# Raw load buffers of a fused linear-attention and feed-forward kernel: rows of 512 bytes instead of 384, three buffers instead of four

## The chip, the cores and the metric

The kernel runs on one core of one Trainium2 chip. The metric is device time in microseconds (us) of one execution. The engines are named as in the profile: PE (TensorE matmul) and PEld (its weight load), DVE (VectorE), ACT (ScalarE), POOL (GpSimd), and SP (SyncE), which here only issues DMAs.

## The reference

The kernel computes a gated linear attention and then a feed-forward layer with a squared ReLU. q, k, v and alpha have shape (4 batches, 8 heads, 768 tokens, 48 channels) in float32; the output is (3072, 384) in float32.

```python
for t in range(S):
    state = alpha[:, :, t, :, None] * state + einsum('bhd,bhe->bhde', k[:, :, t], v[:, :, t])
    y[:, :, t] = einsum('bhd,bhde->bhe', q[:, :, t], state)
x = y.transpose(0, 2, 1, 3).reshape(B * S, H * D)
h = maximum(x @ w_in, 0.0)          # w_in 384 x 2048
out = (h * h) @ w_out               # w_out 2048 x 384
```

## The kernel before, in words

**Tiles.** The work is cut into 12 tiles, numbered g = 0 to 11, of 256 tokens of one batch each. Tiles 0 to 3 are the first parts of the four batches, 4 to 7 the second, 8 to 11 the third. Partition p of the 128 holds the token pair 2p and 2p+1.

**Loads.** For each tile, `load(g)` (L494 to L511) issues four DMAs of 384 KB, for alpha, k, q and v, into one of the raw buffers `RAW` (L378). Such a buffer has, for each partition, the four quantities, each with 8 heads, each with 2 tokens of 48 channels in float32, so that a head has a row of 2 x 48 x 4 = 384 bytes. In HBM the heads of one partition lie far apart, each as a run of 384 bytes. SP issues the loads of all tiles but tile 2, whose four come from POOL (`POOL_LOADS`, L365), as do the four weight loads (`win` and `wout`, L480). Tile g uses buffer g modulo `NRAW` (L367), which is 4.

**What a load waits for.** Three things gate a load: (1) `AFTER` (L1044 to L1046): an earlier transfer must have landed, from tile 4 on the previous tile's q; (2) from tile 5 on, `BEHIND` (L492): an instruction of the previous tile must be done, its Ln for alpha, its k product for k, its transpose for q and v; (3) the buffer must be free: the instructions that read the same part of it for the tile `NRAW` tiles earlier must be done.

**Front of a tile.** `front_by_heads` (tile 0) and `front` (the other tiles) read the raw buffer:
- alpha: Ln on ACT (L525, L587, `la` at L658), the pair product `prd` on DVE or POOL (L616, L618), further products (L645, L654). Cumulated decays come from a TensorE product and Exp on ACT.
- k and q: multiplied with the decays on DVE into `qks` (L561, L687, L692).
- v: cast to bfloat16 into `vbf`, by ACT (L683) or POOL (L554, L682). These two places hold the lines `vin, vout = ...` (L553, L681).

`qks` is then transposed, on TensorE for tiles 0 to 2 and by DMA (L703, issued by SP) from tile 3 on.

**The rest of a tile.** `scores` (L881, masked by DVE at L892), `state` (L752, with L847 to L858) and `output` (L773, L784, L813, L820) make the attention's result `xbf`, which is transposed to `xt` (L927 on TensorE, L933 by DMA). `moe` runs the feed-forward layer: the first product at L983, ReLU at L991 or L993, the square at L1001 or L1005, the second product at L1018, its copy out of PSUM at L1025 or L1027, and a store at L1034. The very last half tile is at L953 to L961. L1068 is filler: TensorE products of zeros in idle time at the start.

**The order of the work.** A list scheduler written in Python (`Program.schedule`) plays the operations through with assumed costs and due times, picks an engine where an operation has alternatives (`alts`), and so fixes the order of instructions on each engine while the kernel is built. `Program.place` turns the dependencies into semaphore waits and drops those that another wait already implies. On the chip each engine runs its list in order, each instruction after its waits.

Of the kernel before, what the change touches and what calls it, by code (L numbers as in the profile page):

```python
# [8 lines left out]
FP32 = mybir.dt.float32  # L9
# [24 lines left out]
class Program:  # L34
# [23 lines left out]
    def add(self, eng, fn, cost, prio, reads=(), writes=(), name="", dma=None, lag=0, after=(), mode=("F", "F"),  # L58
            alts=None):

        reads, writes = ([h for k in keys for h in ((k + (0,), k + (1,)) if len(k) == self.HALVED.get(k[0]) else (k,))]
                         for keys in (reads, writes))
        choices = {eng: (fn, cost)}
        if alts:
            choices.update(alts)
        op = Op(choices, prio, name)
        op.idx = len(self.ops)
        op.lag = lag
        op.mode = mode
        if dma is not None:  # L70
            if dma not in self.dma_sems:
                self.dma_sems[dma] = self.nc.alloc_semaphore("d_" + dma)
                self.dma_count[dma] = 0
            self.dma_count[dma] += 1
            op.sem = (dma, self.dma_count[dma])
        for o in after:
            op.deps[o] = True
        for k in reads:
            w = self.writer.get(k)
            if w is not None:  # L80
                op.deps[w] = True
            if k[0] == "ps":
                for r in self.readers.get(k, ()):
                    op.deps.setdefault(r, False)
        for k in writes:
            w = self.writer.get(k)
            if w is not None:
                op.deps[w] = True
            for r in self.readers.get(k, ()):
                if r is not op:  # L90
                    op.deps.setdefault(r, False)
        for k in reads:
            self.readers.setdefault(k, []).append(op)
        for k in writes:
            self.writer[k] = op
            self.readers[k] = []
        op.deps.pop(op, None)
        self.ops.append(op)
        return op
# [227 lines left out]
def act_ns(n):  # L327
    return 180 + n * 0.8333
# [10 lines left out]
def bass_gla_recurrent__then__act_relu_squared_kernel(  # L339
# [9 lines left out]
    B, H, S, D = q.shape  # L349
# [14 lines left out]
    DENSE = {0: 19172, 1: 35978, 2: 46351, 3: 61182, 11: 160500}  # L364
    POOL_LOADS = {2: "akqv"}  # L365
    RATIO = 4
    NRAW, NQKS, NKQT, NPM, NV, NXT, NGT, NRR, NOSB = 4, 3, 3, 2, 4, 4, 2, 4, 2  # L367
    WS = 2
    LATE_STATE = (1, 2)
    ROW_TILED = tuple(range(PE_TRANSPOSED, G))  # L370
# [4 lines left out]
    def sb(name, shape, dt, n):  # L375
        return [nc.alloc_sbuf_tensor(f"{name}{i}", shape, dt) for i in range(n)]

    RAW = sb("raw", [128, 4, H, 2, D], FP32, NRAW)  # L378
    PRD = sb("prd", [128, HD], FP32, 2)
    LA1 = sb("la1", [128, HD], FP32, 2)  # L380
    LAB = sb("lab", [128, H, 64], BF16, 2)
# [7 lines left out]
    VBF = sb("vbf", [128, H, 2, D], BF16, NV)  # L389
# [104 lines left out]
    def load(g):  # L494
# [7 lines left out]
        for j, t, nm in ((0, alpha, "a"), (1, k, "k"), (2, q, "q"), (3, v, "v")):  # L502
            src = t[b, :, t0:t0 + T, :].rearrange("h (p j) d -> p h (j d)", j=2)
            dst, key = RAW[r][:, j], ("raw", r, j)
            ring, cost, gate = "sp", 600, AFTER.get((g, nm), AFTER.get(g))
# [7 lines left out]
    def front_by_heads(g, p0):  # L513

        r, la, qs, kt, vb = (g % n for n in (NRAW, 2, NQKS, NKQT, NV))
        N = HD // 2

        def lanes(t, x):
            return t[la][:].rearrange("p j (x n) -> p j x n", x=2)[:, :, x]

        for x in range(2):
# [3 lines left out]
            add("act", lambda e, hs=hs: e.activation(LAF[la][:, :, hs, 0:D].rearrange("p j h d -> p h j d"),  # L525
                RAW[r][:, 0, hs], AF.Ln), act_ns(HD) + 30, px + 100, reads=[("raw", r, 0, x)], writes=[("laf", la, x)],
                name=f"ln{x}_{g}")
# [22 lines left out]
            add("act", lambda e, x=x, bank=bank: e.activation(ACM[la][:, 4 * x:4 * x + 4], bank[:, HD:HD + 4], AF.Exp),  # L550
                act_ns(4), p0 + 560 + x, reads=key, writes=[("acm", la, x)], name=f"ec{x}_{g}")

        vin, vout = RAW[r][:, 3].rearrange("p h j d -> p (h j d)"), VBF[vb][:].rearrange("p h j d -> p (h j d)")  # L553
        add("pool", lambda e: e.tensor_copy(vout, vin), 830, p0 + 900, reads=[("raw", r, 3)], writes=[("vbf", vb)],  # L554
            name=f"vc{g}", alts={"act": (lambda e: e.activation(vout, vin, AF.Copy), act_ns(2 * HD))})

        for x in range(2):
            hs = slice(4 * x, 4 * x + 4)
            px = p0 + 40 * x
            for a, E, nm in ((0, EK, "ek"), (1, EQ, "eq")):  # L560
                add("dve", lambda e, a=a, E=E, hs=hs, x=x: e.tensor_tensor(  # L561
                    QKS[qs][:, a, :, hs, 0:D], RAW[r][:, 1 + a, hs].rearrange("p h j d -> p j h d"),
                    lanes(E, x).rearrange("p j (h d) -> p j h d", h=4), ALU.mult), dve_ns(HD), px + 1500 + 10 * a,
# [20 lines left out]
    def decays_by_token(g, p0, r, la):  # L584

        bank, keys = (psX, [("ps", "X", 0), ("ps", "X", 1)]) if g == 0 else (psWH, [("ps", "W"), ("ps", "H", 0)])
        add("act", lambda e: e.activation(LAF[la][:, :, :, 0:D].rearrange("p j h d -> p h j d"), RAW[r][:, 0], AF.Ln),  # L587
            act_ns(2 * HD) + 30, p0 + 100, reads=[("raw", r, 0)], writes=[("laf", la)], name=f"ln{g}")
# [22 lines left out]
    def decays_by_pair(g, p0, r, la, last):  # L611

        def al(j):
            return RAW[r][:, 0, :, j, :]

# [49 lines left out]
    def front(g):  # L665
        b, i = units[g]
        t0 = i * T
        p0 = FRONT.get(g, (g - 1) * P)
        if g in BY_HEADS:
            front_by_heads(g, p0)  # L670
            return
        r, la, qs, kt, pm, vb, x2 = (g % n for n in (NRAW, 2, NQKS, NKQT, NPM, NV, 2))
        first, last = i == 0, i == NST - 1
        sr, sw = 2 * b + i % 2, 2 * b + (i + 1) % 2

        if g in BY_TOKEN:
            decays_by_token(g, p0, r, la)
        else:
            decays_by_pair(g, p0, r, la, last)

        vin, vout = RAW[r][:, 3].rearrange("p h j d -> p (h j d)"), VBF[vb][:].rearrange("p h j d -> p (h j d)")  # L681
        add("pool", lambda e: e.tensor_copy(vout, vin), 830, p0 + 900, reads=[("raw", r, 3)], writes=[("vbf", vb)],  # L682
            name=f"vc{g}", alts={"act": (lambda e: e.activation(vout, vin, AF.Copy), act_ns(2 * HD))})  # L683

        for j in range(2) if g in ROW_TILED else ():
            dst = QKS[qs][:, 1].rearrange("p j h d -> p (j h d)").rearrange("p (n j x d) -> p j n x d", n=NPR, j=2, x=2)[:, j, :, :, 0:D]
            add("dve", lambda e, j=j, dst=dst: e.tensor_tensor(  # L687
                dst, RAW[r][:, 2, :, j, :].rearrange("p (n x) d -> p n x d", x=2),
                EQ[la][:, j].rearrange("p (n x d) -> p n x d", n=NPR, x=2), ALU.mult),
                dve_ns(HD), p0 + 1600 + j, reads=[("raw", r, 2), ("eq", la, j)], writes=[("qks", qs, 1, j)], name=f"eqm{j}_{g}")  # L690
        for a, E, key in ((0, EK, "ek"), (1, EQ, "eq"))[:1 if g in ROW_TILED else 2]:
            add("dve", lambda e, a=a, E=E: e.tensor_tensor(  # L692
                QKS[qs][:, a, :, :, 0:D], RAW[r][:, 1 + a].rearrange("p h j d -> p j h d"),
                E[la][:].rearrange("p j (h d) -> p j h d", h=H), ALU.mult),
                dve_ns(2 * HD), p0 + 1500 + 100 * a, reads=[("raw", r, 1 + a), (key, la, 0), (key, la, 1)],
                writes=[("qks", qs, a)], name=f"{key}m{g}")

        if g in ROW_TILED:

            for c in range(2):  # L700
                src = QKS[qs][64 * c:64 * c + 64].rearrange("p a j h d -> p (a j h d)")
                dst = transposed(kt, c).rearrange("p (b s) -> p b s", s=64)
                add("sp", lambda e, dst=dst, src=src: e.dma_start_transpose(dst, src), 1300, p0 + 2500 + c,  # L703
                    reads=[("qks", qs, 0), ("qks", qs, 1)], writes=[("kqt", kt, 0, c), ("kqt", kt, 1, c)], name=f"tr{c}_{g}",
                    dma=f"t{c}_{kt}", lag=1700)
            return

        for a in range(2):
            src = QKS[qs][:, a].rearrange("p j h d -> p (j h d)")
            bank = psZ[:, a, :].bitcast(BF16)  # L710
            psk = [("ps", "Z", a)]

            def tr(pe, src=src, bank=bank):
                for o in range(2 * NPR):
                    ins = pe.matmul(bank[:, o * 128:(o + 1) * 128], src[:, o * 128:(o + 1) * 128], IDENT[:],
                                    is_transpose=True)
                return ins

            add("pe", tr, pe_ns(8, 128), p0 + 2500 + a, reads=[("qks", qs, a), ("ident",)], writes=psk,
                name=f"tr{a}_{g}")  # L720
            dst = KQT[kt][:, a].rearrange("p j n s -> p (j n s)")
            add("dve", lambda e, dst=dst, bank=bank: e.tensor_copy(dst, bank[:, 0:1024]), dve_ns(1024, 2),
                p0 + 3000 + a, reads=psk, writes=[("kqt", kt, a)], name=f"et{a}_{g}",
                alts={"act": (lambda e, dst=dst, bank=bank: e.activation(dst, bank[:, 0:1024], AF.Copy),
                              act_ns(1024))})
# [374 lines left out]
```

## Time and profile before

| | |
|---|---|
| Time, three runs | 176.28, 176.63, 177.08 us; median 176.63 |
| Profiled execution | span 174.5 us from the first to the last instruction, 5086 instructions; its time beyond the span is not recorded by itself |
| PE busy | 167.6 us (96%) |
| PEld busy | 129.9 us (74%) |
| DVE busy | 121.7 us (70%) |
| ACT busy | 118.9 us (68%) |
| POOL busy | 15.3 us (9%) |
| SP's DMA queue (q1) | 73,184 packets, 28.32 MB, 72.3% of the 16 DMA engines' span |
| POOL's DMA queue (q0) | 1,536 packets, 4.72 MB, 12.2% |
| Raw loads from SP | 44 of 384 KB; median time from issue to landing 3.6 us (alpha), 4.4 (k), 4.0 (q), 4.8 (v) |

How to read it: the profile comes from one execution, seen by the hardware profiler. A group of instructions is named by its line, its engine and "output <- inputs" by the program's tensors, without buffer numbers. "Idle before" is idle time of an engine ahead of these instructions, with what ended it. PE's busy time is modelled from pipelined matmuls, so a busy PE is not necessarily a PE at its peak. SPq is SP's list of DMA issues; an issue can last long when the DMA queues are full.

### The profile page before, as it was taken

The page shows a single profiled execution, that of the slowest core. Times are in us where ns is not written, and L with a number is a line of the kernel's source. Part 1 is how long each engine was busy: PE and PEld are TensorE (multiplying, and loading weights), DVE is VectorE, ACT ScalarE, POOL GpSimd, SP SyncE. Part 2 cuts the span into 40 slices and gives each one's busy share as a digit, 9 for nine tenths or more (in the row PEclk, how much of TensorE's full clock was granted, in tenths as well). Part 3 has the DMA queues.
Part 4 walks back from the last instruction along what each step waited for, and adds up shares of the span by engine and source line. Part 5 has one row for each costly group of instructions (what it writes and reads, how often), then busy time and mean ns, then how long its engine had stood idle before and what let it go on. Part 6 is the DMA issues. An engine that isn't in the chain of part 4 may idle for free.

```text
span 174.5 us, 5086 instructions
## 1 busy us (share of the span) xinstructions
PE 167.6 (96%) x2233; PEld 129.9 (74%) x2235; DVE 121.7 (70%) x201; ACT 118.9 (68%) x211; POOL 15.3 (9%) x24
## 2 busy tenths in 40 slices
PE   7998988999999989999999999999999999999994
PEld 2566887856787669778778878878788797688773
DVE  5597959596958599978869958958769726322230
ACT  3863689777769669578679759669578564566440
POOL 3160840020002002000200000000000000000000
PEclk9999999999999999999999999999999999999999
DMA  5999999989999899899999998899999690040022
GB/s 144 324 296 197 259 307 214 236 213 313 210 226 174 215 232 190 209 246 193 258 199 183 258 193 207 225 191 264 248 186 209 112 187 4 0 135 4 10 80 90
DMA packets 74742, 33.36 MB, mean 191 GB/s; under 512 B 71648, under 2 KB 71904, under 8 KB 74720
## 3 DMA queue, kind: packets, MB, share of 16 engines
q1 hardware_dynamic: 73184, 28.32, 72.3%
q0 software_dynamic: 1536, 4.72, 12.2%
q8 instruction: 17, 0.28, 0.7%
q14 instruction: 5, 0.04, 0.1%
HBM read 25.17 MB, written 4.72 MB: 171 GB/s over the span
## 4 chain that ended last, share of the span: by engine, by line
PE 62%; DMA 27%; SPq 4%; DVE 2%; ACT 2%; POOL 1%; issue 1%
PE psWH L983 27%; PE psO L1018 26%; DMA win<-in_moe_w_in_dram 7%; DMA raw<-in_q_dram 7%; DMA raw<-in_alpha_dram 5%; DMA wout<-in_moe_w_out_dram 4%; DMA raw<-in_v_dram 4%; SPq L509 3%; PE psX L784 2%; PE psX L773 2%; PE psX L953 2%; PE psX L881 1%; PE psZ L752 1%; DVE pm L892 1%; PE psZ L881 1%
## 5 line engine op out<-in xcount | busy, mean ns | idle before, releaser
L983 PE MATMUL psWH<-xt,win 128*128 128x256 bf16 x576 | 73.6, 274 | 1.5 <-DMA win<-in_moe_w_in_dram 1.0
L983 PEld LDWEIGHTS psWH<-xt,win 128*128 128x128 bf16 x576 | 65.2, 145 | 6.5 <-issue 0.8
L1018 PE MATMUL psO<-wout,gt 128*128 128x384 bf16 x368 | 69.4, 326 | 0.1
L991 ACT ACTIVATE rr<-psWH 128x512 bf16<-128x512 f32 x80 | 47.3, 595 | 23.0 <-PE psWH L983 21.4
L1018 PEld LDWEIGHTS psO<-wout,gt 128*128 128x128 bf16 x368 | 34.7, 98 | 18.2 <-ACT osb L1025 0.3
L1001 DVE TENSOR_TENSOR gt<-rr 128x1024 bf16<-128x1024 bf16 (+1 forms) x43 | 25.6, 597 | 24.7 <-ACT rr L991 24.4
L892 DVE TENSOR_TENSOR pm<-psX,caus 128x1024 bf16<-128x1024 f32 x12 | 14.6, 1218 | 0.9 <-PE psZ L881 0.9
L892 DVE TENSOR_TENSOR pm<-psZ,caus 128x1024 bf16<-128x1024 f32 x12 | 14.6, 1218 | 0.8 <-PE psZ L881 0.8
L1005 ACT ACTIVATE gt<-rr 128x512 bf16<-128x512 bf16 (+1 forms) x17 | 14.1, 828 | 0.5
L912 ACT ACTIVATE xbf<-psX 128x768 bf16<-128x768 f32 x12 | 9.7, 810 | 6.4 <-PE psX L773 5.4
L1025 ACT ACTIVATE osb<-psO 128x384 f32<-128x384 f32 x19 | 9.3, 492 | 5.7 <-PE psO L1018 5.1
L993 DVE TENSOR_SCALAR rr<-psWH 128x512 bf16<-128x512 f32 x16 | 11.0, 688 | 1.6 <-PE psWH L983 0.8
L687 DVE TENSOR_TENSOR qks<-raw,eq 128x384 bf16<-128x384 f32 x18 | 10.0, 589 | 2.4 <-DMA raw<-in_q_dram 2.4
L683 ACT ACTIVATE vbf<-raw 128x768 bf16<-128x768 f32 x10 | 8.4, 841 | 3.6 <-DMA raw<-in_v_dram 3.5
L1068 PE MATMUL psO<-zero 128*128 128x512 bf16 (+1 forms) x33 | 9.3, 417 | 1.4 <-DVE zero L430 1.3
L692 DVE TENSOR_TENSOR qks<-raw,ek 128x768 bf16<-128x768 f32 x11 | 10.4, 950 | 0.0
L847 DVE TENSOR_TENSOR smd<-psZ,sbd 128x384 bf16<-128x384 f32 x8 | 4.5, 557 | 5.3 <-PE psX L773 5.3
L1068 PEld LDWEIGHTS psO<-zero 128*128 128x128 bf16 x35 | 3.4, 108 | 4.9 <-issue 1.9
L658 ACT ACTIVATE la<-raw 128x384 f32<-128x384 f32 x8 | 4.2, 522 | 4.3 <-DMA raw<-in_alpha_dram 4.3
L645 DVE TENSOR_TENSOR ek<-ek,raw 128x384 f32<-128x384 f32 x10 | 5.6, 557 | 1.2 <-ACT ek L636 1.1
L636 ACT ACTIVATE ek<-psWH 128x384 f32<-128x384 f32 x10 | 4.9, 490 | 1.4 <-PE psWH L628 1.4
L619 ACT ACTIVATE lab<-prd 128x384 bf16<-128x384 f32 x10 | 5.2, 520 | 0.7 <-DVE prd L616 0.6
(115 smaller groups left out, 156.8 us busy)
## 6 DMA issues: line engine op xcount, KB each, us to landing
raw<-in_alpha_dram SPq DMA_DIRECT2D x11, 384.0 KB, 3.6
raw<-in_k_dram SPq DMA_DIRECT2D x11, 384.0 KB, 4.4
raw<-in_q_dram SPq DMA_DIRECT2D x11, 384.0 KB, 4.0
raw<-in_v_dram SPq DMA_DIRECT2D x11, 384.0 KB, 4.8
out_dram<-osb SPq DMA_DIRECT2D x11, 384.0 KB, 4.0
win<-in_moe_w_in_dram POOLq DMA_DIRECT2D x2, 768.0 KB, 10.0
wout<-in_moe_w_out_dram POOLq DMA_DIRECT2D x2, 768.0 KB, 8.4
raw<-in_alpha_dram POOLq DMA_DIRECT2D x1, 384.0 KB, 5.5
```

The source lines that it names most:

```text
L687: add("dve", lambda e, j=j, dst=dst: e.tensor_tensor(dst, RAW[r][:, 2, :, j, :].rearrange("p (n x) d -> p n x d", x=2), EQ[la][:, j].rearr ...
L692: add("dve", lambda e, a=a, E=E: e.tensor_tensor(QKS[qs][:, a, :, :, 0:D], RAW[r][:, 1 + a].rearrange("p h j d -> p j h d"), E[la][:].rear ...
L892: add("dve", lambda e, hf=hf, psT=psT: e.tensor_tensor(PM[pm][:, hf].rearrange("p r n j t -> p (r n) (j t)"), psT[:, :, :].rearrange("p r ...
L912: add("act", lambda e: e.activation(XBF[x2][:], psX[:, :, 0:HD], AF.Copy), act_ns(2 * HD), p0 + 6100, reads=[("ps", "X", 0), ("ps", "X", 1 ...
L983: ins = pe.matmul(psH[hb][:, i * T:(i + 1) * T], WIN[:, kk, hidden(fj)], mov, start=(kk == 0), stop=(kk == KT - 1))
L991: add("act", lambda e, hb=hb, rr=rr: e.activation(rr, psH[hb], AF.Relu), act_ns(512), pu + 600, reads=[("ps", "H", hb)], writes=[("rr", rb ...
L993: alts={"dve": (lambda e, hb=hb, rr=rr: e.tensor_scalar(rr, psH[hb], 0.0, None, ALU.max), dve_ns(512))})
L1001: add("dve", lambda e, dst=dst, sq=sq: e.tensor_tensor(dst, sq, sq, ALU.mult), 148 + k * 267, pu + 1200, reads=[("rr", rb, h) for h in ran ...
L1005: "act": (lambda e, dst=dst, sq=sq: e.activation(dst, sq, AF.Square), act_ns(k * 512))})
L1018: ins = pe.matmul(psS, GT[gt][:, fj, j, :], WOUT[:, fj, :], start=(fj == 0), stop=(fj == FT - 1))
L1025: add("act", lambda e, j=j, psS=psS: e.activation(OSB[ob][:, j], psS, AF.Copy), act_ns(DM), ps_ + 700, reads=[keyS], writes=[("osb", ob, j ...
L1068: pr.fill(lambda n: lambda pe: pe.matmul(psO[:, 0:n], ZERO[:, 0:128], ZERO[:, 0:n], skip_group_check=True), ((512, 216, 420), (256, 109, 2 ...
```

## The change

A head's row in a raw buffer takes 128 float32 (512 bytes) of which the first 96 are used, and there are three raw buffers instead of four. The raw buffers together keep their size: 4 x 4 x 8 x 384 bytes = 3 x 4 x 8 x 512 bytes = 49,152 bytes for each partition. As a whole quantity is no longer one unbroken run, the two casts of v read and write it head by head. The loads, which are written as 128 x 8 x 96 elements in both kernels, get the new row step through `RAW` itself. All lines after the buffers stand two lines lower in the changed kernel.

```diff
-    NRAW, NQKS, NKQT, NPM, NV, NXT, NGT, NRR, NOSB = 4, 3, 3, 2, 4, 4, 2, 4, 2
+    NRAW, NQKS, NKQT, NPM, NV, NXT, NGT, NRR, NOSB = 3, 3, 3, 2, 4, 4, 2, 4, 2
...
-    RAW = sb("raw", [128, 4, H, 2, D], FP32, NRAW)
+    PITCH = 128
+    RAW = [t[:, :, :, 0:2 * D].rearrange("p a h (j d) -> p a h j d", j=2)
+           for t in sb("raw", [128, 4, H, PITCH], FP32, NRAW)]
...
-        vin, vout = RAW[r][:, 3].rearrange("p h j d -> p (h j d)"), VBF[vb][:].rearrange("p h j d -> p (h j d)")
+        vin, vout = RAW[r][:, 3].rearrange("p h j d -> p h (j d)"), VBF[vb][:].rearrange("p h j d -> p h (j d)")
```

The last pair of lines stands twice, in `front_by_heads` and in `front`.

More of the change, by code (lines that the diff above doesn't have):

```diff
@@ L679, in front @@
             decays_by_pair(g, p0, r, la, last)
-        vin, vout = RAW[r][:, 3].rearrange("p h j d -> p (h j d)"), VBF[vb][:].rearrange("p h j d -> p (h j d)")
+        vin, vout = RAW[r][:, 3].rearrange("p h j d -> p h (j d)"), VBF[vb][:].rearrange("p h j d -> p h (j d)")
         add("pool", lambda e: e.tensor_copy(vout, vin), 830, p0 + 900, reads=[("raw", r, 3)], writes=[("vbf", vb)],
```

## The prediction

> **What bounds the kernel now.** I read the chain of work that ended last first, because it says where the end comes from. The shares by engine, then pieces of its list in order of time (columns: start in us, length in us, what):
>
> ```profile
> PE 62%; DMA 27%; SPq 4%; DVE 2%; ACT 2%; POOL 1%; issue 1%
> ```
>
> ```profile
> 4.26 4.84 DMA raw<-in_alpha_dram
> ...
> 31.18 6.55 DMA raw<-in_q_dram
> ...
> 39.72 6.72 DMA raw<-in_v_dram
> ...
> 46.47 0.84 ACT vbf L683
> ...
> 47.98 4.68 DMA raw<-in_alpha_dram
> ...
> 55.47 5.22 DMA raw<-in_q_dram
> ...
> 60.71 1.03 DVE qks L687 x2
> ```
>
> Until 64.5 us the chain hops from load to load, with the two weights between them; from 64.53 us to the end it is TensorE almost without a break. So the end is "when TensorE stops being starved" plus fixed TensorE work, and the change touches no TensorE instruction. The list has five pieces of raw loads, 28.0 us together.
>
> Next the table of stages (stage, its length, then busy us per engine with counts, clock, DMA share, GB/s), for how much starvation there is to win back:
>
> ```profile
> 4.30:9.10 4.80, 4.73 (x51) 2.71 (x51) 2.64 (x6) 3.59 (x9) 0.96 (x1) 1.00 1.17 324
> ...
> 37.70:46.50 8.80, 8.37 (x116) 5.92 (x114) 7.21 (x14) 6.36 (x15) 0.00 (x0) 1.00 1.14 250
> ...
> 55.50:64.50 9.00, 8.18 (x102) 5.60 (x94) 6.99 (x12) 5.75 (x13) 0.00 (x0) 1.00 0.87 224
> 64.50:153.20 88.70, 88.60 (x1264) 71.00 (x1265) 67.05 (x102) 63.82 (x112) 2.31 (x2) 1.00 0.89 188
> ```
>
> PE looks busy everywhere, but its weight loads show the density: 71.00/88.70 = 80% in the steady stage, 67% and 62% in two early ones. Against 80%, the stages from 30.1 to 64.5 us hold about 4 us of lost TensorE time. That is the most that faster loads could return there. The clock is 1.00 throughout.
>
> The loads are bound by the queues: with nothing else to wait for, SP issues one 384 KB load every 1.19 us. In the timeline (start, length, what):
>
> ```profile
> 4.26 1.15 SPq L509 DMA_DIRECT2D raw<-in_alpha_dram  x1
> 5.46 1.15 SPq L509 DMA_DIRECT2D raw<-in_k_dram  x1
> 6.65 1.15 SPq L509 DMA_DIRECT2D raw<-in_q_dram  x1
> ```
>
> A load is 1,024 pieces of 384 bytes, 64 per DMA engine, so 1.19 us / 64 = 18.6 ns per piece.
>
> **The change, part by part.** *Order.* The built program has the same instructions in the same order on all five engines. No DMA is added, and total raw memory stays 4 x 12,288 = 3 x 16,384 = 49,152 bytes, so no other tensor moves. What is left is waits, addresses and access patterns.
>
> *Waits from three buffers.* Only the four loads of tile 4 get new ones: they now overwrite tile 1 instead of tile 0, and wait for tile 1's Ln, its two products and its V copy. In the timeline these end at 9.97, 13.68, 14.55 and 13.78 us; the loads issue from 37.75 us, once tile 3's q has landed. The margin is 23 us. From tile 5 on the loads keep their gates (previous tile's q landed, previous tile's Ln, product or transpose done), which imply the reuse condition; the tightest is tile 5's alpha, 47.98 us against tile 2's last alpha read at 29.24 us. The cost is one extra wait instruction on SP ahead of tile 4's alpha. The trace has such a lone wait at 47.92 us: 17 ns, the next issue 65 ns after its start. It lies on the chain, and behind it on SP stand tile 4's loads, the first store and the transposes. I take +0.07 us. The other three waits ride on issues that also run as long with a wait as without (0.59 and 0.58 us): 0.
>
> *Addresses: the load's pieces.* The destination is 1,024 pieces of 384 bytes in both kernels, because the heads lie apart in HBM. Only where a piece starts changes. The built program puts the first raw buffer at byte 16,512 = 32 x 512 + 128 of a partition. So before, heads start at 128, 0, 384, 256 past a 512-byte line, in turn; after, all eight start at 128. (The rows step by 512 bytes but do not start on a 512-byte line.) All four starts are thus in the trace already, a quarter of the pieces each, and the new one is among them. The trace's DMA packet records say what they cost: of 45,056 pieces of 384 bytes on SP's queue, 43,822 (97.3%) lasted exactly 22 ns; the next commonest, 523, lasted 20. Even if all the others were of one start, nine tenths of that start lasted 22 ns too. I take 0. From both sides: the fastest rate in the records is that of the 3,072-byte stores, 121 ns, or 15.1 ns per 384 bytes, against 18.6 paced. If the mean 18.6 hid a cheap half at 15.1, the dear half would be 22.1. So a load's packet time could change by (15.1 - 18.6)/18.6 = -19% to +19%.
>
> What that is worth on the chain: the five pieces hold 4 loads (up to tile 1's alpha), 3 (tile 3 up to q), 4 (tile 4), 1 and 1, the rest being latency, weights, stores and transposes in the same queues. 13 loads x 1.19 us = 15.5 us, of which 19% is 2.9 us.
>
> [...]
>
> *The four loads that POOL issues for tile 2.* Their shape stays 128 x 8 x 96 and they were already written piece by piece (packet sizes 4,224 and 3,456 bytes, multiples of 384 and not of 3,072). POOL's issue rows, 0.89 to 0.95 us, stay: 0.
>
> *Access patterns.* 54 DVE instructions, 8 on ACT and 3 on POOL already step over rows of 384 bytes and will step 512. The other 13 ACT reads and 2 POOL casts of a whole row block go from one run of 768 (or 384) to eight (or four) runs of 96. For stepping itself the groups by line give the nearest rows (busy us, mean ns):
>
> ```profile
> L658 ACT ACTIVATE la<-raw 128x384 f32<-128x384 f32 x8 | 4.2, 522 | 4.3 <-DMA raw<-in_alpha_dram 4.3
> L525 ACT ACTIVATE laf<-raw 128x384 bf16<-128x384 f32 x2 | 0.9, 514 | 0.9 <-DMA raw<-in_alpha_dram 0.9
> L616 DVE TENSOR_TENSOR prd<-raw 128x384 f32<-128x384 f32 x7 | 3.9, 553 | 0.3 <-DMA raw<-in_alpha_dram 0.2
> L858 DVE TENSOR_TENSOR sbd<-tmp,acm 128x384 bf16<-128x384 f32 x6 | 3.3, 555 | 0.1
> ```
>
> ACT reads eight stepped runs in 522 ns and the unbroken run in 514: 8 ns. DVE's stepped 553 equals its unbroken 555. I take +8 ns per ACT copy; one `vbf` is on the chain: +0.01 us. POOL's first cast (962 ns, at 7.93 us) releases TensorE's state product at 8.97 us; its cost lies between 0 and, by POOL's dearest cast of this form (1,084 ns), +0.12 us. It is covered: the second tile's scores end at 17.21 us and TensorE then waits until 17.49 us for the first weight, 0.28 us of slack. Without that cover it would cost its 0.12 us. Whether a step of 512 is dearer than one of 384 no row shows: rival C.
>
> *Sum.* 0.07 + 0 + 0 + 0.01 = +0.08 us on a span of 174.5, so 174.6. The profiled execution is known by its span; the median 176.63 is 2.1 us above it, which I carry over: **176.7 us**.
>
> **The rivals.**
>
> *A, slower: the off-boundary start is dear.* If a piece that starts 128 bytes past a 256-byte boundary takes longer, after the change every piece does. Place: the load pieces of the chain before 64.5 us. [...] It decides as soon as a load issue on SP takes longer than 1.15 us. For it: half of today's pieces start on a boundary, none will. Against it: one duration for all.
>
> *B, faster: crossing a 512-byte line is dear.* Before, the starts at 256 and 384 make half of the pieces cross such a line; after, none does. Price at most -2.9 us, **173.7 us**, within the 4 us that TensorE can regain. Against it, again: one duration. For it: packet records may not show a cost that is paid at landing.
>
> *C, slower: a step of 512 bytes slows the engines' reads.* The nearest dear row is POOL, 997 ns for the product that DVE does in 553: +80%. On the chain that adds 0.67 (`vbf`), 0.82 (`qks` twice) and 0.80 us (POOL's `prd`): **178.9 us**. After 64.5 us it stays hidden: 3.2 us of such DVE reads per tile would grow by 2.5, and DVE idles 24% of a 12.5 us tile, 3.0. For it: no row has this step. Against it: 384 against no step costs 0 to 8 ns.
>
> *D, slower: a third buffer too few.* The margins above, 18.7 us and more, leave it only a few hundredths of a us; a load would have to be 18 us early.
>
> **How the numbers follow.** My forecast has chance 0.60, A 0.12, B 0.16, C 0.10, D 0.02. About 0.5% (0.9 us) is what a measurement of this kernel can tell from no change. So faster 0.16, same 0.60, slower 0.24. The forecast's own range is 176.1 to 177.5 (the runs of before spread over 0.8 us). To leave out no more than 2 in 10 I reach into B down to 174.6 and into A and C up to 179.4.
>
> **What would show it.** Right: 384-byte pieces still at 22 ns, SP's early issues at 1.15 us, ACT's `vbf` copies at 842 ns give or take 10, one more wait on SP near 37.7 us, the TensorE-only part of the chain again from 64 to 65 us. A shows as issues of up to 1.4 us; B as issues below 1.1 us or earlier landings at equal issues; C as longer `qks` and `vbf` rows; D as SP idle before a load on a DVE or ACT row. I would be wrong if a landing, or an engine's read, depends on the start of a row in a way that no packet record and no row of this profile carries.

## The result and the profile after

| | before | after |
|---|---|---|
| median, runs of the first comparison | 176.95 us (20) | 178.31 us (20) |
| lowest and highest | 175.45, 182.14 us | 176.30, 180.94 us |
| ratio, 95% interval | | 1.0075 (1.0049 to 1.0101) |
| span of the profiled execution | 174.5 us | 177.1 us |

The time was forecast as 176.7 us, within 174.6 to 179.4. The kernel came out 0.75% slower in this comparison, 0.44% and 0.05% in two repeats (below). Ratios leave out every run that took over 1.5% more than the fastest of its kernel, medians do not.

First the chain of work that ended last, shares by engine:

```profile
PE 61%; DMA 27%; SPq 5%; DVE 2%; ACT 2%; POOL 1%; issue 1%
```

Then its pieces (start in us, length in us, what):

```profile
4.21 5.11 DMA raw<-in_alpha_dram
...
10.54 12.98 DMA win<-in_moe_w_in_dram
23.81 8.01 DMA wout<-in_moe_w_out_dram
...
41.81 6.04 DMA raw<-in_v_dram
49.34 5.84 DMA raw<-in_alpha_dram
...
57.75 5.50 DMA raw<-in_q_dram
63.28 1.03 DVE qks L689 x2
```

In the kernel before, the two weights (`win`, `wout`) on this chain read:

```profile
10.32 11.94 DMA win<-in_moe_w_in_dram
22.55 7.58 DMA wout<-in_moe_w_out_dram
```

It is the same chain of loads, but `qks` starts at 63.28 us instead of 60.71: all 2.6 us of the longer span are there by this point. They come in small parts. Tile 1's alpha landed at 9.32 us instead of 9.10. The first weight then took 12.98 us on the chain instead of 11.94, the second 8.01 instead of 7.58, tile 5's alpha 5.84 instead of 4.68.

The table of stages (stage, length, busy us and counts of PE, PEld, DVE, ACT, POOL, then clock, DMA share, GB/s), for the 88.7 us behind the chain's last load, 2.6 us later than in the kernel before:

```profile
67.10:155.80 88.70, 88.63 (x1264) 71.01 (x1265) 66.41 (x102) 63.85 (x113) 2.05 (x2) 1.00 0.90 188
```

TensorE's and ACT's times agree with those of before within 0.03 us (88.60, 71.00, 63.82): nothing was lost after the start. Next, SP's early issues:

```profile
4.21 1.42 SPq L511 DMA_DIRECT2D raw<-in_alpha_dram  x1
5.67 1.15 SPq L511 DMA_DIRECT2D raw<-in_k_dram  x1
6.86 1.15 SPq L511 DMA_DIRECT2D raw<-in_q_dram  x1
8.06 1.15 SPq L511 DMA_DIRECT2D raw<-in_v_dram  x1
```

Three still take 1.15 us; one took 1.42, which is how alpha came 0.2 us late. (The first two issues of the program, with no load and one load ahead of them, took 0.46 and 0.56 us in both kernels.) An issue of up to 1.4 us was the prediction's sign of rival A, but one alone does not bear it out: issues of 1.33 and 1.40 us also stand among the loads with 384-byte rows in the run of loads alone (below). In the packet records 43,653 of 45,056 pieces of 384 bytes lasted 22 ns (before: 43,822). Then the groups by line (out<-in, shapes, count | busy us, mean ns | idle before):

```profile
L689 DVE TENSOR_TENSOR qks<-raw,eq 128x384 bf16<-128x384 f32 x18 | 9.4, 555 | 4.9 <-DMA raw<-in_q_dram 4.6
L685 ACT ACTIVATE vbf<-raw 128x768 bf16<-128x768 f32 x10 | 8.4, 842 | 6.4 <-DMA raw<-in_v_dram 6.4
L660 ACT ACTIVATE la<-raw 128x384 f32<-128x384 f32 x8 | 4.2, 522 | 6.4 <-DMA raw<-in_alpha_dram 6.4
```

Two of the same groups in the kernel before (that of `la` stands in the prediction; a mean of 589 comes from one product of 1,179 ns, the others take 553):

```profile
L687 DVE TENSOR_TENSOR qks<-raw,eq 128x384 bf16<-128x384 f32 x18 | 10.0, 589 | 2.4 <-DMA raw<-in_q_dram 2.4
L683 ACT ACTIVATE vbf<-raw 128x768 bf16<-128x768 f32 x10 | 8.4, 841 | 3.6 <-DMA raw<-in_v_dram 3.5
```

ACT and DVE did not read the wider rows more slowly (`vbf` 842 ns against 841, `la` 522 against 522, `qks` 555 against 553); what grew is the idle time until a load lands, for instance 6.4 us ahead of `la` instead of 4.3. Last, SP around tile 4, where the third buffer adds its waits:

```profile
36.02 1.15 SPq L511 DMA_DIRECT2D raw<-in_v_dram  x1
39.69 0.37 SPq L511 DMA_DIRECT2D raw<-in_alpha_dram  x1
40.10 0.58 SPq L511 DMA_DIRECT2D raw<-in_k_dram  x1
```

Alpha and k are issued 0.41 us apart, as before (37.75 and 38.16 us); no reader of tile 1 is waited for. The trace has the one extra wait instruction on SP at 37.22 us, 17 ns long, 2.47 us ahead of alpha's issue: it was over before tile 3's q landed at 39.68 us, and alpha's issue started 16 ns after that landing, as in the kernel before. So one pair of profiles says: the arrivals of the first 63 us were late, by no cause that the profile names. The experiments ask whether the lateness belongs to the change (theory 1: the longer row step costs, somewhere) or to the run (theory 2: arrivals vary, and a pair of profiles shows luck).

### The profile page after: what moved, and what is told of

The parts are those of the page before. It is cut to its first block, busy times and chain, and to the rows that moved or that the text cites. A ratio compares the mean times of both kernels' runs of the same rounds, so it can differ in the third digit from the quotient of the medians.

```text
span 177.1 us, 5087 instructions
## 1 busy us (share of the span) xinstructions
PE 168.5 (95%) x2233; PEld 130.7 (74%) x2235; DVE 121.1 (68%) x201; ACT 119.1 (67%) x211; POOL 15.2 (9%) x24
## 4 chain that ended last, share of the span: by engine, by line
PE 61%; DMA 27%; SPq 5%; DVE 2%; ACT 2%; POOL 1%; issue 1%
PE psWH L985 26%; PE psO L1020 25%; DMA win<-in_moe_w_in_dram 7%; DMA raw<-in_alpha_dram 6%; DMA raw<-in_v_dram 6%; DMA wout<-in_moe_w_out_dram 5%; SPq L511 4%; DMA raw<-in_q_dram 3%; PE psX L786 2%; PE psX L775 2%; PE psX L955 1%; PE psX L883 1%; PE psZ L754 1%; DVE pm L894 1%; ACT vbf L685 1%; PE psZ L883 1%
## 5 line engine op out<-in xcount | busy, mean ns | idle before, releaser
L1003 DVE TENSOR_TENSOR gt<-rr 128x1024 bf16<-128x1024 bf16 (+1 forms) x43 | 25.6, 596 | 26.1 <-ACT rr L993 25.9
L689 DVE TENSOR_TENSOR qks<-raw,eq 128x384 bf16<-128x384 f32 x18 | 9.4, 555 | 4.9 <-DMA raw<-in_q_dram 4.6
L754 PE MATMUL psZ<-vbf,qks 64*128 64x96 bf16 x144 | 5.6, 202 | 0.0
## 6 DMA issues: line engine op xcount, KB each, us to landing
win<-in_moe_w_in_dram POOLq DMA_DIRECT2D x2, 768.0 KB, 11.1
```

Source lines behind the costliest of these rows:

```text
L689: add("dve", lambda e, j=j, dst=dst: e.tensor_tensor(dst, RAW[r][:, 2, :, j, :].rearrange("p (n x) d -> p n x d", x=2), EQ[la][:, j].rearr ...
L1003: add("dve", lambda e, dst=dst, sq=sq: e.tensor_tensor(dst, sq, sq, ALU.mult), 148 + k * 267, pu + 1200, reads=[("rr", rb, h) for h in ran ...
```

## The experiments

**Both kernels again.** The kernel before, unedited, timed against itself, and the changed kernel, unedited.

> The kernel before, unchanged, as a second profile and as a yardstick: ratio 1.000 within about 0.3%. In the first pair of profiles win took 11.94 us on the chain before and 12.98 after, and all 2.6 us of difference arose before TensorE's unbroken stretch (64.5 against 67.1 us). If those 1.0 us on win are luck of one execution, this profile should show win anywhere between 11.9 and 13.0 and the stretch starting between 64.5 and 66.5; if win is tied to the layout, it stays at 11.9 to 12.2.

> The changed kernel, unchanged, as a second profile: ratio 1.005 to 1.010. If the layout slows a fixed step, the same step is late again: POOL's first cast 1.12 us instead of 0.96, the first weight again about 1 us late, tile 2's packets from POOL at 211 ns in the middle instead of 188. If the late steps are others, then the profile pair differed mostly by luck, and the timed ratio alone carries the effect.

| | this kernel, median (12 runs) | before (35 runs) | ratio, 95% interval | span of its profile |
|---|---|---|---|---|
| kernel before | 177.87 us | 177.00 us | 0.9972 (0.9922 to 1.0023) | 177.1 us |
| changed kernel | 178.48 us | 177.00 us | 1.0044 (1.0006 to 1.0083) | 176.7 us |

The kernel before has a profile of 177.1 us too: its first one, 174.5 us, was a lucky one. The first weight took 10.96 us in this second profile (issued at 10.23 us, landed at 21.19) and 10.81 us in the changed kernel's second, less than in either first profile, so late weights do not belong to the layout. And the changed kernel's second profile has no early loss. The first mask product of tile 4 (`pm`), a milestone behind the last load of the chain, starts at 62.1 us in both profiles of the kernel before, at 64.7 us in the first of the changed kernel and at 62.1 us in the second (61.6 to 62.2 us in the four later profiles with 512-byte rows). **The 2.6 us of the first pair of profiles do not come from the change.** The second profile lost its time later. This is its chain of work around tile 10:

```profile
119.61 6.09 DMA raw<-in_q_dram
...
125.71 4.44 DMA raw<-in_alpha_dram
...
130.18 0.57 DVE prd L618
...
130.77 0.52 ACT lab L621
...
132.53 1.53 PE psWH L985 x12
```

Tile 10's q took 6.09 us (in the first profile of before 3.75, from issue to the next alpha's issue, which waits for it), tile 11's alpha was held back behind it, and TensorE waited for its decays. From tile 9's first mask product to tile 10's it took 14.5 us instead of 12.5. The kernel before loses time in the same step in its second profile, 14.4 us, there behind a DMA transpose (`xt<-xbf`, 4.94 us on its chain).

**One half of the change at a time.** First the row step of 512 with four buffers:

```diff
-    RAW = sb("raw", [128, 4, H, 2, D], FP32, NRAW)
+    PITCH = 128
+    RAW = [t[:, :, :, 0:2 * D].rearrange("p a h (j d) -> p a h j d", j=2)
+           for t in sb("raw", [128, 4, H, PITCH], FP32, NRAW)]
```

(with the two casts of v as in the change), then three buffers of 384-byte rows:

```diff
-    NRAW, NQKS, NKQT, NPM, NV, NXT, NGT, NRR, NOSB = 4, 3, 3, 2, 4, 4, 2, 4, 2
+    NRAW, NQKS, NKQT, NPM, NV, NXT, NGT, NRR, NOSB = 3, 3, 3, 2, 4, 4, 2, 4, 2
...
+    sb("gap", [128, 4, H, 2, D], FP32, 1)
```

> Rows of 512 bytes with four raw buffers; everything behind the buffers lies 16,384 bytes further up, with the same start modulo 512. If the row step (loads, reads or the split casts) costs the 0.75%: ratio 1.0075, as the change itself. If three buffers cost it: 1.000. If each has a part, in between.

> Three raw buffers with rows of 384 bytes, and the fourth buffer's place left empty, so that all other tensors stay where they are; tile 4's loads get the same new waits as in the change. If the waits of three buffers cost the 0.75%: ratio 1.0075. If the row step does: 1.000, or 1.0004 for the one lone wait (0.07 us) on the chain.

Measured, 12 runs each beside the same 35 of before: the row step alone 177.93 us, ratio 1.0035 (0.9998 to 1.0073), profiled span 176.1 us; three buffers alone 177.38 us, 1.0005 (0.9967 to 1.0044), profiled span 176.0 us. Three buffers cost nothing that can be measured. The row step is where a cost would be, but its interval still holds 1.

**The loads alone.** Nothing but DMAs: groups of sixteen loads on SP's queue, each group with another layout, three times; then groups of four on POOL's queue.

```python
LAYOUTS = ((96, 32), (128, 32), (128, 0), (112, 32))   # row step, start past a 512-byte line, in float32
for rep in range(REPS):
    for step, at in LAYOUTS:
        for i in range(N):
            e.dma_start(slot(i, step, at), source(i)).then_inc(done, 16)
        n += N
        e.wait_ge(done, 16 * n)
```

> DMAs alone, no attention and no feed-forward layer (the output is zeros). SP issues 16 raw loads back to back, waits for all, and repeats with four layouts in turn, three times: rows of 384 bytes from 128 past a 512-byte line (as before), of 512 bytes from 128 past (as changed), of 512 bytes from the line itself, and of 448 bytes. Then POOL issues four loads at a time with the same layouts. If a piece's start is dear (rival A): the second layout up to 19% longer than the first, the third shorter. If crossing a 512-byte line is dear (rival B): the second shorter than the first. If the layout is free, as forecast: all four about 16 x 1.19 = 19.0 us plus one landing of about 2 us, alike within 1%, and POOL's alike too. If an unbroken destination is what made the old rows cheap: the first layout shorter than the three others.

| rows | starts past a 512-byte line | 16 loads, first issue to last packet, us | 384-byte packets at 22 ns |
|---|---|---|---|
| 384 (before) | 128, 0, 384, 256 | 21.56, 22.71, 21.41 | at least 98.7% |
| 512 (after) | 128 | 21.10, 21.24, 21.22 | at least 98.7% |
| 512 | 0 | 21.13, 22.27, 21.15 | at least 98.7% |
| 448 | every second one 64 off a multiple of 128 | 23.23, 23.18, 23.13 | 43%, mean 25.6 ns |

Here rows of 512 bytes loaded as fast as rows of 384, if anything 1% faster (21.10 to 21.24 us against 21.41 and 21.56), and it made no difference whether they started on a line or 128 bytes past it (21.13 and 21.15 us against 21.10 to 21.24).

(Two of the twelve groups, 22.71 and 22.27 us, took 5 to 6% longer than others of their layout; the profile names no reason, and they are left out of this comparison.) Of the layouts tried only the one with every second start 64 bytes off a multiple of 128 was slower, by 8 to 10% (23.13 to 23.23 us), which was not foreseen. POOL's groups of four took 7.0 to 7.75 us from first issue to last packet in the first three layouts. With rows of 448 bytes they took 10.7 to 11.1 us, but each of these groups holds a pause of 3.5 to 4.6 us between two of POOL's issues, which comes after every fifteenth load of the run, so they say nothing of the layout. This ends rivals A and B for loads with no other work beside them.

**The loads among transposes and stores.** The order of a steady tile on SP's queue, DMAs alone. First groups of three tiles with three layouts, then five pairs of groups with the two layouts of the two kernels, then 42 tiles without a break, one layout per kernel, timed:

```python
for i in (0, 1):
    e.dma_start(slot(4 * t + i, STEP, START), source(4 * t + i)).then_inc(done[t], 16)
for c in range(2):
    e.dma_start_transpose(kqt[2 * t + c][:, 0:1024].rearrange("p (b s) -> p b s", s=64),
                          qks[64 * c:64 * c + 64, :]).then_inc(done[t], 16)
e.dma_start(rows(tile % 12), osb[:]).then_inc(done[t], 16)
for i in (2, 3):
    e.dma_start(slot(4 * t + i, STEP, START), source(4 * t + i)).then_inc(done[t], 16)
e.dma_start_transpose(xt[t][:], xbf[:]).then_inc(done[t], 16)
```

> DMAs alone again (the output is zeros), in the order of a steady tile on SP's queue: two raw loads, two transposes of qks, a store of 384 KB, two raw loads, a transpose of xbf; three such tiles, then a wait for all; three layouts in turn, three times. (The first four groups carry the stores, the rest none, so groups are compared only with groups of the same content.) If the new rows slow loads, or the transposes and stores beside them, only when the queue is mixed: the layouts of 512 bytes longer than that of 384 by more than 1%. If the layout is free here too: alike within 1%, and the 0.5% of the whole kernel must come from somewhere other than the queue's own speed.

> DMAs alone: the order of loads, transposes and stores of three steady tiles, ten times, five with rows of 384 bytes and five with rows of 512 in turn, all starts as in the two kernels; nothing is computed, the output is zeros. The earlier run had one clean pair of such groups: 33.57 against 34.44 us. Theory 1 by way of the shared queue: the 512-byte groups are longer by 0.5 to 0.9 us on average, with transposes' 256-byte packets at 23 to 25 ns against 21.5. Theory 2: the mean of the five differs by less than 0.3 us, and the order of the pairs is mixed.

> DMAs alone, nothing is computed, the output is zeros: 42 steady tiles in the kernel's order on SP's queue (two loads, two transposes, a store, two loads, a transpose), three tiles in flight, with rows of 384 bytes. The ten earlier groups of three tiles took 33.3 us with these rows and 33.9 us with 512 on average, single pairs from -0.5 to +1.9 us. At 33.3 less 1.5 us of draining per group I expect some 445 us here; what counts is the difference from the run that follows. Theory 1 by way of the shared queue: the run with 512-byte rows is longer by 1.6%, some 7 us. Theory 2: they differ by less than 2 us (0.4%) either way.

> The same 42 tiles of DMAs alone (nothing is computed, the output is zeros) with rows of 512 bytes, all starting 128 bytes past a 512-byte line as in the changed kernel. Theory 1 by way of the shared queue: some 7 us longer than with rows of 384 bytes, which in the kernel, whose first 64 us wait on DMAs, would be +0.6 to +1 us, the size of what the comparisons show. Theory 2: within 2 us of it; then the queue is not the place, and the 0.5% would have to come from the way in which the engines' reads and the arrivals fall together.

The first kernel gave 33.57 and 33.67 us for a group with 384-byte rows and 34.44 and 34.38 us with 512 (from 128 past a line, and from the line): a promising 0.8 us. (Its groups without stores, 28.63 us with 384 against 28.14 to 29.03 us with 512, showed no such gap.) The second kernel blurred it: 33.49, 33.67, 32.87, 34.12, 32.56 us with 384 against 34.48, 33.19, 34.79, 34.54, 32.43 with 512. The pairs differ by +0.99, -0.48, +1.92, +0.42 and -0.13 us, mean +0.54, which so few pairs cannot tell from zero. The long kernels settled it: median **463.98 us** (460.86 to 467.26, six runs) with 384-byte rows, **464.11 us** (461.99 to 467.99, six runs) with 512, where theory 1 wanted 7 us more. (Both are longer than the 445 us that was expected; the comparison does not need that figure.) The line of DMA packets on the page of the first, then of the second:

```profile
DMA packets 303075, 112.91 MB, mean 243 GB/s; under 512 B 297696, under 2 KB 297696, under 8 KB 303072
```

```profile
DMA packets 303075, 112.91 MB, mean 244 GB/s; under 512 B 297696, under 2 KB 297696, under 8 KB 303072
```

The same packets at the same rate; the 0.8 us of the first groups did not come back. With this spread a difference under 3 us (0.6%) would not be seen (an estimate from the two sets of six runs). On the 64 us of the kernel that wait for DMAs, 0.6% is 0.4 us, so a slower shared queue, with no engine at work beside it, cannot carry the 0.9 us that the kernels differ by (next section).

**The changed kernel a third time, its rows moved to a line, and its v unbroken.** The second has no more than two spacers around the raw buffers:

```diff
+    sb("gap", [128, 96], FP32, 1)
     RAW = [t[:, :, :, 0:2 * D].rearrange("p a h (j d) -> p a h j d", j=2)
            for t in sb("raw", [128, 4, H, PITCH], FP32, NRAW)]
+    sb("rest", [128, 32], FP32, 1)
```

In the third, v's quarter of a buffer keeps unbroken rows:

```diff
-    RAW = [t[:, :, :, 0:2 * D].rearrange("p a h (j d) -> p a h j d", j=2)
-           for t in sb("raw", [128, 4, H, PITCH], FP32, NRAW)]
+    class Raw:
+        def __init__(self, t):
+            self.t = t
+
+        def __getitem__(self, i):
+            t, j = self.t, i[1]
+            if j == 3:
+                x = t[:, 3, 0:H * 2 * D].rearrange("p (h x) -> p h x", x=2 * D)
+            else:
+                x = t[:, j].rearrange("p (h x) -> p h x", x=PITCH)[:, :, 0:2 * D]
+            x = x.rearrange("p h (j d) -> p h j d", j=2)
+            return x[(i[0],) + tuple(i[2:])]
+
+    RAW = [Raw(t) for t in sb("raw", [128, 4, H * PITCH], FP32, NRAW)]
```

> The changed kernel as it is, once more, beside the two edits of it that follow. Two comparisons so far gave it 0.75% and 0.44% over the kernel before, with 512-byte rows in four buffers 0.35% and three buffers of 384-byte rows 0.05%. Theory 1 (the longer row step itself costs 0.5 to 0.75%): a ratio of 1.004 to 1.008 again. Theory 2 (the row step costs nothing, and what the comparisons saw is the luck of DMA arrivals, which moved single profiled spans from 174.5 to 177.1 us): a ratio that is as often below 1.003 as above, and this run ends nearer to 1.000.

> The changed kernel with its raw buffers moved by 384 bytes, so that every head's row starts on a 512-byte line and not 128 bytes past it; all tensors allocated after them move by 512 bytes. [...] Theory 1 (the step costs, whatever the start): the changed kernel's ratio, give or take 0.003. Theory 2 (nothing but luck): 1.000 give or take 0.004. The loads alone gave 21.13 and 21.15 us for sixteen of them from a line against 21.10 and 21.24 us from 128 bytes past it, so I expect no difference from the changed kernel.

> The changed kernel with only v's quarter of each raw buffer laid out as before, in unbroken rows of 384 bytes; alpha, k and q keep the step of 512. All V copies on ACT and POOL read one run again. Theory V (the V copies carry the cost: POOL's first one took 1,123 ns in the changed kernel and 962 in the kernel before, and the second TensorE stage waits behind it): the ratio falls to 1.000 give or take 0.003, and POOL's first copy is back at 960 ns. Theory 1 in its form of loads and stepped reads: the ratio stays that of the changed kernel of this job, at most a quarter lower. Theory 2: no difference beyond 0.004 from either.

| 12 runs each, beside 29 of before (177.00 us) | median | ratio, 95% interval | span of its profile |
|---|---|---|---|
| changed kernel | 177.69 us | 1.0005 (0.9964 to 1.0046) | 176.1 us |
| rows start on a line | 177.45 us | 1.0020 (0.9980 to 1.0060) | 175.2 us |
| v unbroken | 178.62 us | 1.0055 (1.0014 to 1.0096) | 175.1 us |

The line start is no remedy that can be told from the changed kernel. Neither is the unbroken v: POOL's first copy did come back, as the timelines show, first of the changed kernel's first profile and then of this one (start, length, what, idle before):

```profile
8.14 1.12 POOL L556 CAST vbf<-raw 128x768 bf16<-128x768 f32 x1 [5.19 <-DMA raw<-in_v_dram]
```

```profile
7.92 0.98 POOL L569 CAST vbf<-raw 128x768 bf16<-128x768 f32 x1 [4.98 <-DMA raw<-in_v_dram]
```

but the time did not; theory V falls. The profiled executions of the last two kernels were quick ones, 176.91 and 176.83 us against medians of 177.45 and 178.62.

**What the nine profiles of whole kernels say together.** Three have rows of 384 bytes (174.5, 177.1, 176.0 us; mean 175.9), six rows of 512 (177.1, 176.7, 176.1, 176.1, 175.2, 175.1; mean 176.05). The means agree, but with single spans 2.6 us apart nine profiles are too few to show a difference of 0.9 us. All nine need 27.7 us from tile 11's first mask product to the end. They differ in when loads land, and much in loads during which a packet of 16,384 bytes runs on the instruction queue q8. The first profile of before and the second of the changed kernel, in the window from the issue of tile 10's q to that of the next alpha:

```profile
GB/s 426 426 309 137 123 156 178 208 199 128 115 139 109 153 246 247 227 159 153 180 205 131 184 262 303 279 324 319 328 328 316 287 266 303 279 466 307 307 307 307
...
q8 instruction: 1, 0.02, 1.5%
```

```profile
GB/s 383 235 126 205 228 217 176 182 137 94 76 71 118 146 219 249 285 287 305 410 270 300 302 302 307 305 320 287 202 81 48 20 20 20 20 20 20 20 20 20
...
q8 instruction: 1, 0.02, 1.0%
```

The rate is given in 40 slices. In the first, 307 GB/s hold to the end. In the second the last 9 slices, 1.4 us, run at 20 GB/s, a sixteenth of 307: **by the rate (an estimate), one of the 16 DMA engines was still at work there and the load waited for it.** The q8 packets take 0.88 to 2.0 us each, 17 in a run.

In the nine profiles the loads of q of tiles 6 and 8, which never have one beside them, take 3.47 to 4.44 us to the next alpha's issue, those of tiles 5 and 10, which always have one, 3.75 to 6.10 us. Tile 7's q took 3.93 to 5.81 us in the seven profiles where it had one, 3.92 and 4.23 us in the two where it had none. That is a correlation. The packet in the second window lasted 0.93 us, less than the 1.4 us at 20 GB/s, and the trace does not name the engine on which a packet ran, so it is not shown that the packet made this load late.

Whether a load on the path to TensorE pays for such a packet here stays open. The 42-tile kernels, which are short programs, have no such packet in their records.

## Why the prediction came out as it did

*The bound and where a loss would be.* Right in the first part: until about 64 us the end is set by when loads feed TensorE. Too simple in the second: the work behind it is not fixed. The 88.7 us stretch is the same to 0.03 us in the first pair of profiles, but these two are exceptions. From tile 4's first mask product to the end it took 112.4 us in both, and 112.8 to 115.0 us in the other seven, of both row steps, because TensorE waited for DMAs again, mostly in the step from tile 9 to tile 10: in six of the seven the chain there holds tile 10's q and tile 11's alpha behind it, in one a DMA transpose. The prediction priced all its rivals on the loads before 64.5 us alone, so a loss in later transfers had no place in its sum.

*Order, waits, three buffers.* Right that three buffers cost nothing: 1.0005 with three buffers alone. The lone wait's +0.07 us, nearly all of the sum, was wrong: the wait does not lie on the chain. It runs at 37.22 us, while SP has yet to wait for tile 3's q, and the issue behind that landing starts 16 ns after it in both kernels; the term is 0. Rival D falls.

*Pieces, 0.* Right, with the working behind it: one packet duration, 22 ns, for all four starts, in the whole kernel and in the loads alone. Rivals A and B fall. Their price of up to 2.9 us supposed that the mean of 18.6 ns hides two kinds of pieces; sixteen loads with one start took as long as sixteen with all four (21.10 to 21.24 us against 21.41 and 21.56), so it hides none.

*Reads, +0.01.* Right: ACT's `vbf` copies took 842 ns against 841, its `la` 522 against 522, DVE's 768-wide `qks` 948 against 950. Rival C falls. POOL's first copy was given 0 to +0.12 us on 0.96. With 512-byte rows it took 1.12, 0.97 and 1.14 us in the changed kernel, 1.23 with the row step alone and 0.92 from a line; with 384-byte rows 0.96, 0.94 and 0.82, with v unbroken 0.98. That is up to +0.27 us, so the term was mis-sized at its upper end; it was covered: in the profile with 1.23 us tile 4's first mask product started at 61.8 us, before the 62.1 us of the kernel before. And v with its old rows gave no time back that can be told. What the row step has to do with it is doubtful, since this copy meets a DVE product (last section).

*Sum, +0.08 us, and own range 176.1 to 177.5.* Here the forecast failed in the first comparison: 178.31 us, 1.36 us over the kernel before, outside its own range. It lies inside the whole range, up to 179.4, only because that leaves room for rivals A and C, and neither happened; that is luck.

Part of the gap may be chance: the three ratios of the changed kernel are 1.0075, 1.0044 and 1.0005, mean 1.0041, or 0.7 us. It is not all chance. The six ratios of kernels with 512-byte rows are 1.0075, 1.0044, 1.0005, 1.0035, 1.0020 and 1.0055, all above 1, mean 1.0039; the two with 384-byte rows are 0.9972 and 1.0005, mean 0.9989. Several of the eight share their runs of the kernel before, and by the medians that kernel stood 0.5% above itself (177.87 against 177.00 us), so it is safer to pool every execution (three buffers of 384-byte rows count with the kernel before). In the three sets of runs the kernels with 512-byte rows took 178.40, 178.35 and 178.08 us in the mean and those with 384-byte rows 177.20, 177.44 and 177.36 us: 1.2, 0.9 and 0.7 us more, together 0.9 us (an estimate; 0.5 to 1.3 us by resampling the runs). So a cost near 0.5% goes with the row step, and the steps of the prediction have no term for it: what they give for the row step, pieces 0 and reads +0.01 us, comes to nothing.

**What stays open** is its cause. Spoken against by a run: the pace of loads, alone or (to 0.6%) among transposes and stores, the start of a row, the third buffer, the v copies. Spoken against by rows: the engines' reads, and a steady slowing of loads while engines work beside them, since the q of tiles 6 and 8 took 3.94 us to the next alpha's issue on average with 384-byte rows and 3.92 with 512.

What is left, and was not tried, is how loads, instruction packets and the engines' work fall together. In tile 10, q to the next alpha took 3.75, 4.61 and 4.47 us in the three profiles with 384-byte rows and 3.97, 6.10, 5.10, 5.44, 5.50 and 5.86 with 512: means 4.28 and 5.33. The step to tile 10's first mask product follows it: 12.5 us in the two profiles where that q took under 4 us, 13.1 to 14.5 us in the six where it took 4.47 us or more and stands on the chain. But over all profiles this step differs less, 13.3 us on average (12.5, 14.4, 13.1) against 13.6 (12.5, 14.5, 13.3, 13.9, 13.7, 13.7), and a pattern found in nine profiles after the fact is no test. A test would be a kernel whose packets on q8 fall at other times while its loads stay.

*A step on the way.* The prediction carried 2.1 us from the profiled span to the median. The later runs have their spans beside their times, 1.7 us apart (177.1 and 178.82); so that execution took some 176.2 us, and was a quick one among 20 with a median of 176.95. Measured against it, most second profiles look slow.

## What to carry to other kernels

Before a difference of one pair of profiles is explained, take a second profile of each kernel: here the spans of one kernel differ by 2.6 us, more than the effect, and the first explanation, late weights, was gone in the second. Put a suspected DMA cost into a kernel of DMAs alone and repeat it enough: three tiles showed +0.8 us where 42 showed +0.1 of 464. Among the loads alone, of 384-byte pieces, row steps of 384 and 512 bytes took the same within about 2% (21.41 and 21.56 us against 21.10 to 21.24), while a step of 448 bytes, which puts every second start 64 bytes off a multiple of 128, took 23.13 to 23.23 us, 8 to 10% more. And a chain of work read from one profile shows where that execution waited: here the chain had no load on it after 64.5 us, and in seven of nine profiles TensorE waited for DMAs again later.

## What the runs showed of the hardware

*The end of one load ran at a sixteenth of the rate.* In the second profile of the changed kernel the last 1.4 us of tile 10's q stood at 20 GB/s, a sixteenth of 307: by the rate (an estimate), one of the 16 DMA engines was still at work. That load took 6.10 us, and 3.97 in another profile of the same kernel.

*The kernel before has a spread of its own.* Its median was 176.95 and 177.00 us beside the runs above and 178.36 us (11 runs) beside the 42-tile kernels: the sets of runs differ by more than the change makes, so only runs of one set are compared.

*Where POOL's copy met DVE's product, one of the two or both took longer.* In the profile of before, tile 7's two meet (start, length):

```profile
85.67 1.65 DVE L687 TENSOR_TENSOR qks<-raw,eq 128x384 bf16<-128x384 f32 x2
```

```profile
85.82 1.08 POOL L682 CAST vbf<-raw 128x768 bf16<-128x768 f32 x1 [17.31 <-DMA raw<-in_v_dram]
```

DVE's pairs took 1.02 to 1.11 us elsewhere in this profile (the median product 553 ns); here one product took 1,179 ns. POOL's copy took 1.08 us here and 0.82 where they do not meet, as at 90.47 us in the changed kernel. The same was seen at about 8 us, between POOL's first copy and a product of tile 0. In the second profile of before, with three buffers alone and with the rows on a line, DVE's product was the long one, 1,177 to 1,195 ns, POOL's copy took 0.82 to 0.94 us, and tile 0's first mask product started at 11.0 us; in the other six it was POOL's copy that was long, 0.96 to 1.23 us, and the mask product started at 10.0 to 10.7 us. By tile 4 the difference is gone (61.7 to 63.2 us against 61.6 to 64.7). So at about 8 us one of the two was long in every profile; by what mechanism is not shown.
